# Decode attention on one core: scores of the next head before the PV of this one, K queued ahead of V, a replicated q layout, and a new start

## The chip, the cores and the metric

The kernel runs on one core of one Trainium2 chip. Times are device microseconds of a whole execution. The engines are called PE (matmul), PEld (weight load), DVE (vector), ACT (scalar), POOL (GpSimd) and SP (the sequencer that here issues nearly all DMAs).

## The reference

There are two independent blocks, A and B, with the same shapes; their outputs are joined. Each is one decode step of attention with a long cache:

```python
B, Sq, D = 8, 1, 1024;  H, Sk, Dh = 32, 4096, 128        # bf16
q = (x @ wq).reshape(B, Sq, H, Dh).transpose(0, 2, 1, 3)
scores = einsum("bhqd,bhkd->bhqk", q, k_cache) * Dh ** -0.5
o = einsum("bhqk,bhkd->bhqd", softmax(scores), v_cache)
out = o.transpose(0, 2, 1, 3).reshape(B, Sq, H * Dh) @ wo
```

Every byte of K and V is used once: 2 x 2 x 8 x 32 tiles of 1 MB, 1024 MiB, plus 32 MiB of wq and wo.

## The kernel before

A "head" n (64 in all, both blocks in a row) is 8 batches. For each batch one K tile and one V tile of [128, 4096] bf16 (1 MB) are loaded. DVE transposes the K tile; PE makes scores from it (8 matmuls of 512 columns); after eight tiles there is one softmax for all eight batches; then PE does PV (8 matmuls a tile). All loads come from one in-order queue, SP:

```python
NK = 6; NT = 2; NV = 8; LEAD = 2        # K buffers, transposed K, V buffers, q groups ahead

# SP: the load queue
load_group(first[0])                     # wq, eight DMAs of 128 KB, rows of 1 KB
wait(sp, s_const, 1)                     # all GpSimd constants ready
for blk in range(NBLK):
    sp.dma_start(x_sb[0:Bsz, blk, :], blocks[blk][0][:, 0, :]).then_inc(s_x, 16)
for n in range(NH):
    for b in range(Bsz):                 # K of this head
        wait(sp, s_tr, t - NK + 1)       # the transpose that frees the slot
        sp.dma_start(knat[:, slot, :], kc[b, h]...).then_inc(s_kld[slot], 16)
    for G in groups_at.get(n, []): load_group(G)
    sp.dma_start(wo_sb[:, ws, :], wo[h * 128:(h + 1) * 128, :])...
    for b in range(Bsz):                 # V of this head
        wait(sp, s_pv, t - NV + 1)       # the PV that frees the slot
        sp.dma_start(vnat[:, slot, :], vc[b, h]...).then_inc(s_vld[slot], 16)

# POOL: ahead of s_const
pool.memset(x_sb[:], 0.0)                # 128 partitions, of which 8 are used
pool.memset(q_pad[:], 0.0)
pool.memset(lpad[:], 0.0)
... # the constants, ident among them, then s_const

# PE, for head n
scores(n); max, bias and sum matmuls of n; prep(n + 1); PV(n); transpose o; output projection
# ... cut: the code is inline, in this order

# ACT, eviction of PV and the output
act.wait_ge(s_pv, (n + 1) * Bsz)         # all eight PV tiles
for slot in range(2):
    act.activation(o_sb[:, slot, :], O_ps[slot], ACT.Identity, scale=rlo_sb[:, slot:slot + 1])
...
for c in range(NOC):                     # last head of a block: NOC = 2 copies
    act.activation(out_sb[32 * c:32 * c + 8, blk, :], OUT_ps[c], ACT.Identity)
```

## Time and profile before

| | before |
|---|---|
| median (4 runs before the prediction; 13 with those taken beside the changed kernel) | 2669.84 us; 2669.67 us |
| profiled span | 2667.8 us |
| PE / DVE / ACT busy | 75% / 48% / 10% |
| read from HBM | 1107.33 MB, 415 GB/s over the span |
| last V tile landed | 2660.23 us |

The table of the span in 40 equal slices comes first. A digit of 9 means that the mean of the 16 DMA engines was busy for 90% or more of the slice; GB/s is what they moved. The last line is the share of each engine in the chain of work that ended last.

```profile
DMA  9999999999999999999999999999999999999998
GB/s 371 418 420 421 417 421 417 421 420 416 420 416 420 421 417 420 415 421 420 415 420 417 421 419 416 420 413 420 419 419 421 414 421 414 419 420 418 421 421 349
...
DMA 80%; DVE 9%; SPq 7%; PE 2%; issue 1%; ACT 0%; POOL 0%; DVEq 0%; POOLq 0%; ACTq 0%
```

Between the first and the last slice the rate never leaves 413 to 421 GB/s. This kernel's engines idle at every softmax (38.5 to 41.8 us in the first head), and its DMA rate does not show it: it is bound by its loads. Both ends are lower. The start, cut into stretches of 2.5 us, shows why (start and end, length, busy us and instructions of five engines, granted PE clock, DMA share, GB/s):

```profile
0.00:2.50 2.50, 0.00 (x0) 0.00 (x0) 1.40 (x3) 0.00 (x0) 1.91 (x5) 1.00 0.18 45
2.50:5.00 2.50, 0.00 (x0) 0.00 (x0) 2.22 (x6) 0.00 (x0) 2.50 (x3) 1.00 0.86 262
5.00:7.50 2.50, 0.00 (x0) 0.00 (x0) 0.26 (x1) 0.00 (x0) 2.47 (x6) 1.00 0.36 113
7.50:10.00 2.50, 0.00 (x0) 0.00 (x0) 0.83 (x5) 0.00 (x0) 0.80 (x6) 1.00 0.05 13
10.00:12.50 2.50, 0.39 (x32) 0.33 (x32) 0.00 (x0) 1.50 (x2) 0.00 (x0) 1.00 0.93 315
12.50:15.00 2.50, 2.44 (x38) 0.96 (x39) 1.26 (x1) 0.23 (x2) 0.00 (x0) 1.00 1.01 426
```

POOL is busy with memsets until 8 us, SP waits for it with x and K behind, and the DMA falls to 13 GB/s. The last part, from the timeline (start, length, engine, line, operation), runs from the last V tile to the issue of the output:

```profile
2660.27 1.89 PE L372 MATMUL ps<-vnat,pq_sb 128*4 128x512 bf16 x8 [0.57 <-DMA vnat<-in_B_v_cache_dram]
2662.20 1.26 ACT L452 ACTIVATE o_sb<-ps,rlo_sb 128x512 bf16<-128x512 f32 x2 [15.23 <-PE ps L372]
...
2664.56 1.20 ACT L460 ACTIVATE out_sb<-ps 8x512 bf16<-8x512 f32 x2 [0.48 <-PE ps L394]
2665.79 0.63 ACTq L463 DMA_DIRECT2D out_dram<-out_sb  x2
```

### The profile page before, as it was taken

What the parts mean: (1) busy time and instruction counts of PE and PEld (TensorE: products, weight loads), DVE (VectorE), ACT (ScalarE), POOL (GpSimd) and SP (SyncE); (2) the same over time, 40 slices, a digit from 0 to 9 for tenths busy, and PEclk for the clock granted to TensorE, in tenths of its full rate; (3) what the DMA queues carried; (4) which work ended last, traced back from release to release, by engine and by line L of the source; (5) the groups of instructions that cost most, each with busy time, mean ns of one, the idle gap of its engine ahead of it and who ended that gap; (6) DMA issues with size and microseconds to landing.
All of it is one profiled execution on the core that took longest, in us unless ns stands there. A gap on an engine that the chain in (4) does not pass through costs nothing.

```text
span 2667.8 us, 26152 instructions
## 1 busy us (share of the span) xinstructions
PE 2010.0 (75%) x10880; PEld 729.4 (27%) x10880; DVE 1292.2 (48%) x781; ACT 263.2 (10%) x727; POOL 7.7 (0%) x17
## 2 busy tenths in 40 slices
PE   6777777777777777777777777777777777777777
PEld 2222222222222222222222222222222222222222
DVE  5453544545535445364453544535535355363553
ACT  1001100011000110110101101011010100101001
POOL 1000000000000000000000000000000000000000
PEclk9998999999989999999999999999999899999999
DMA  9999999999999999999999999999999999999998
GB/s 371 418 420 421 417 421 417 421 420 416 420 416 420 421 417 420 415 421 420 415 420 417 421 419 416 420 413 420 419 419 421 414 421 414 419 420 418 421 421 349
DMA packets 175316, 1109.09 MB, mean 416 GB/s; under 512 B 19504, under 2 KB 35920, under 8 KB 44128
## 3 DMA queue, kind: packets, MB, share of 16 engines
q1 hardware_dynamic: 175136, 1107.41, 100.5%
q8 instruction: 86, 1.41, 0.2%
q14 instruction: 30, 0.25, 0.0%
q10 hardware_dynamic: 64, 0.03, 0.0%
HBM read 1107.33 MB, written 0.03 MB: 415 GB/s over the span
## 4 chain that ended last, share of the span: by engine, by line
DMA 80%; DVE 9%; SPq 7%; PE 2%; issue 1%; ACT 0%; POOL 0%; DVEq 0%; POOLq 0%; ACTq 0%
DMA knat<-in_B_k_cache_dram 39%; DMA knat<-in_A_k_cache_dram 36%; DVE kt L249 9%; SPq L189 3%; DMA vnat<-in_B_v_cache_dram 3%; DMA vnat<-in_A_v_cache_dram 3%; SPq L171 2%; SPq L202 1%; PE ps L334 1%; PE ps L289 1%; PE ps L372 0%; SPq L197 0%; ACT o_sb L452 0%; POOL lpad L211 0%; PE ps L394 0%
## 5 line engine op out<-in xcount | busy, mean ns | idle before, releaser
L249 DVE STREAM_TRANSPOSE kt<-knat 128x2048 f32<-128x2048 f32 x512 | 1171.2, 2304 | 1119.1 <-DMA knat<-in_B_k_cache_dram 536.6
L334 PE MATMUL ps<-kt,lpad 128*128 128x512 bf16 x4096 | 1025.1, 395 | 227.0 <-DVE kt L249 225.4
L372 PE MATMUL ps<-vnat,pq_sb 128*4 128x512 bf16 x4096 | 848.0, 432 | 121.7 <-DMA vnat<-in_B_v_cache_dram 60.7
L334 PEld LDWEIGHTS ps<-kt,lpad 128*128 128x128 bf16 x4096 | 368.0, 99 | 876.2 <-DVE kt L249 445.5
L372 PEld LDWEIGHTS ps<-vnat,pq_sb 128*4 128x4 bf16 x4096 | 292.2, 94 | 647.4 <-issue 151.2
L452 ACT ACTIVATE o_sb<-ps,rlo_sb 128x512 bf16<-128x512 f32 x128 | 80.9, 683 | 881.6 <-PE ps L372 881.6
L437 ACT ACTIVATE bias_sb<-ps 128x1 f32<-128x1 f32 x64 | 11.0, 171 | 1363.5 <-PE ps L347 1363.5
L253 DVE TENSOR_REDUCE m_sb<-ps 128x1 bf16<-128x512 f32 x64 | 44.4, 694 | 128.7 <-PE ps L334 128.7
L383 PE MATMUL ps<-selrow,o_sb 128*128 128x4 bf16 x512 | 22.6, 166 | 86.9 <-ACT o_sb L452 86.9
L261 DVE STREAM_TRANSPOSE pq_sb<-e_sb 128x512 bf16<-128x512 bf16 x64 | 45.5, 712 | 83.7 <-ACT e_sb L441 83.7
L424 ACT ACTIVATE lpad<-ps 32x32 bf16<-32x32 f32 x256 | 77.9, 304 | 70.3 <-PE ps L306 65.6
L354 PE MATMUL ps<-l1m_sb,maskcg 128*32 128x2 f32 x512 | 16.4, 188 | 90.5 <-ACT l1m_sb L445 90.5
L342 PE MATMUL ps<-ident,m_sb 128*1 128x128 bf16 x64 | 13.9, 217 | 50.3 <-DVE m_sb L253 50.3
L383 PEld LDWEIGHTS ps<-selrow,o_sb 128*128 128x128 bf16 x512 | 17.0, 96 | 119.0 <-ACT o_sb L452 119.0
L441 ACT ACTIVATE e_sb<-ps,bias_sb 128x512 bf16<-128x512 f32 x64 | 44.0, 687 | 2.1
L289 PE MATMUL ps<-wq_sb,xT_sb 128*8 128x512 bf16 x128 | 37.8, 449 | 0.0
L394 PE MATMUL ps<-wo_sb,oT_sb 128*8 128x512 bf16 x128 | 24.9, 386 | 17.1 <-ACT oT_sb L456 17.1
L354 PEld LDWEIGHTS ps<-l1m_sb,maskcg 128*32 128x32 f32 x512 | 10.9, 117 | 96.0 <-ACT l1m_sb L445 96.0
L306 PE MATMUL ps<-ident,q_pad 128*32 128x8 bf16 x1024 | 17.4, 171 | 24.9 <-DVE rlo_sb L264 24.2
L347 PE MATMUL ps<-scalecol,negm 128*32 128x1 bf16 x256 | 12.0, 177 | 23.9 <-DVE negm L257 23.9
L257 DVE TENSOR_REDUCE negm<-ps 1x16 bf16<-1x128 f32 x64 | 18.0, 281 | 19.8 <-PE ps L342 19.8
L342 PEld LDWEIGHTS ps<-ident,m_sb 128*1 128x1 bf16 x64 | 5.1, 79 | 82.1 <-DVE m_sb L253 82.1
(37 smaller groups left out, 119.2 us busy)
## 6 DMA issues: line engine op xcount, KB each, us to landing
knat<-in_A_k_cache_dram SPq DMA_DIRECT2D x256, 1024.0 KB, 26.4
vnat<-in_A_v_cache_dram SPq DMA_DIRECT2D x256, 1024.0 KB, 20.8
knat<-in_B_k_cache_dram SPq DMA_DIRECT2D x256, 1024.0 KB, 26.5
vnat<-in_B_v_cache_dram SPq DMA_DIRECT2D x256, 1024.0 KB, 20.9
wq_sb<-in_A_wq_dram SPq DMA_DIRECT2D x64, 128.0 KB, 10.1
wo_sb<-in_A_wo_dram SPq DMA_DIRECT2D x32, 256.0 KB, 12.8
wq_sb<-in_B_wq_dram SPq DMA_DIRECT2D x64, 128.0 KB, 9.3
wo_sb<-in_B_wo_dram SPq DMA_DIRECT2D x32, 256.0 KB, 12.8
```

Source lines behind the costliest of these rows:

```text
L171: sp.dma_start(wq_sb[:, G % 2, ch, :], wq[ch * 128:(ch + 1) * 128, g * GW:(g + 1) * GW]).then_inc(s_wq[G % 2], 16)
L189: sp.dma_start(knat[:, slot, :], kc[b, h].rearrange("(p j) d -> p (j d)", p=128),).then_inc(s_kld[slot], 16)
L249: dve.transpose(kt[:, ts, :].bitcast(F32), knat[:, ks, :].bitcast(F32)).then_inc(s_tr, 1)
L253: dve.tensor_reduce(m1_sb[:], S_ps[par], axis=AX.X, op=ALU.max).then_inc(s_m1, 1)
L261: dve.transpose(pq_sb[:], e_sb[:]).then_inc(s_pq, 1)
L289: last = pe.matmul(q_ps[G % 2], lhsT=xT_sb[:, blk, ch, :], rhs=wq_sb[:, G % 2, ch, :], start=(ch == 0), stop=(ch == NCH - 1))
L334: last = pe.matmul(S_ps[par], lhsT=lpad[:, b, c, 2 - 2 * g:2 - 2 * g + 128], rhs=ktv[:, 16 * g:16 * g + 16, bq, :, e_], start=(b == 0 and ...
L372: last = pe.matmul(O_ps[slot][32 * cg:32 * cg + 4, :], lhsT=pq_sb[:, base:base + 97:32], rhs=vnat[:, vs, j0 * 128:(j0 + 4) * 128], start=( ...
L383: last = pe.matmul(oT_ps[:, slot * 4:slot * 4 + 4], lhsT=o_sb[:, slot, m * 128:(m + 1) * 128], rhs=selrow4[:, m, :], start=(m == 0), stop= ...
L424: act.activation(dst, src, ACT.Identity).then_inc(s_lp, 1)
L441: act.activation(e_sb[:], S_ps[par], ACT.Exp, bias=bias_sb[:], scale=SCALE, accum_out=l1_sb[:]).then_inc(s_exp, 1)
L452: act.activation(o_sb[:, slot, :], O_ps[slot], ACT.Identity, scale=rlo_sb[:, slot:slot + 1]).then_inc(s_oev, 1)
```

## The change

The stated intent is to let the engines work on two heads at a time: PE does the scores and the maximum of head n+1 before the PV of head n, K of head n+1 is queued ahead of V of head n, and q is laid out so that four matmuls instead of sixteen prepare a head. The same diff also changes the start, the wq loads and the end:

```diff
-NT = 2
-NV = 8
-LEAD = 2
+NT = 4
+NV = 6
+LEAD = 3
@@ buffers
-        x_sb = sb("x_sb", [128, NBLK, D], BF16)
+        x_sb = sb("x_sb", [8, NBLK, D], BF16)          # no zero fill needed
-        q_pad = sb("q_pad", [128, 2, GW], BF16)
+        q_rep = sb("q_rep", [128, 2, HPG, 4, 128], BF16)
-        rlo_sb = sb("rlo_sb", [128, 2], F32)           # likewise pq_sb: two of each now
+        rlo_sb = sb("rlo_sb", [128, 2, 2], F32)
@@ SP: wq in one DMA, x and K at once, K a head ahead
-                for ch in range(NCH):
-                    sp.dma_start(wq_sb[:, G % 2, ch, :],
-                                 wq[ch * 128:(ch + 1) * 128, g * GW:(g + 1) * GW]).then_inc(s_wq[G % 2], 16)
+                sp.dma_start(wq_sb[:, G % 2, :, :],
+                             wq.rearrange("(ch p) n -> p ch n", p=128)[:, :, g * GW:(g + 1) * GW]
+                             ).then_inc(s_wq[G % 2], 16)
-            load_group(first[0]); wait(sp, s_const, 1); x; K(0), V(0), K(1), V(1), ...   (abridged)
+            x; load_group(first[0]); K(0); then per n: K(n+1), wq, wo, V(n)                (abridged)
@@ POOL: only what is needed, ident first; ACT zeroes q_rep and lpad
@@ PE
+            for n in range(NH):
+                if n + 1 < NH:
+                    qk(n + 1)
+                    smax_a(n + 1)
+                for b in range(Bsz):
+                    pv(n, b)
+                if n + 1 < NH:
+                    smax_b(n + 1)
+                if n + 2 < NH:
+                    prep(n + 2)
+                otr(n)
+                outproj(n)
@@ ACT: each slot is evicted after its own four PV tiles; one output copy; eight small q copies
-                act.wait_ge(s_pv, (n + 1) * Bsz)
                 for slot in range(2):
+                    act.wait_ge(s_pv, m * Bsz + min(4 * (slot + 1), Bsz))
-                    for c in range(NOC):
-                        act.activation(out_sb[32 * c:32 * c + 8, blk, :], OUT_ps[c], ACT.Identity).then_inc(s_outsb, 1)
+                    act.activation(out_sb[0:npart, blk, :], ps[0:npart, 7, 0:OW], ACT.Identity).then_inc(s_outsb, NOC)
... # cut: fp32 operands in the max path, masks moved, PSUM banks renumbered
```

## The prediction

> **What bounds the kernel now.** The DMA engines. The 40-slice table shows DMA at 90% or more in every slice but the last, and 413 to 421 GB/s in all but the first (371) and last (349). 1107 MB come from HBM in 2667.8 us. In 2.5 us stretches around 1000 us, DMA share is 1.00 to 1.04 through three heads, softmax included; the only dip (385, 307, 400 GB/s, about 1 us lost) is a wq group with its 1 KB rows. The chain of waits is 80% DMA. The Trainium skill, "DMA: Bandwidth & Descriptors", section "Where 436 GB/s comes from", puts the fabric ceiling at 435 GB/s; the trace's 419 to 423 is close to it: nothing is left to win in the steady state.
>
> PE (75% busy), DVE (48%) and ACT (10%) have slack: a head needs about 41.5 us of DMA, against 8x1.9 us scores and 8x1.9 us PV on PE (31 us) and 8x2.31 us transposes on DVE.
>
> **What the change does, and what it is worth**
>
> 1. Head pipelining (scores of n+1 before PV of n, later reciprocal, two pq, NT 4): removes idle time around softmax (38.5 to 41.8 us in the timeline, about 3.4 us a head). It is hidden already: about 0 us.
> 2. K(n+1) queued before V(n), NV 8 to 6 (12 MB of slots instead of 14): V(n,6) can only be issued after PV(n,0), which I put about 8.4 us after the last K tile lands (transpose 2.3, scores 1.9, max/row/bias about 2, PV 1.9), with about 15 us of V queued. Some 6 us remain, so no steady bubble: 0 us.
> 3. Start. Before, x waits for GpSimd memsets until 8.4 us and K begins at 9.1 us; by 10 us only 1.08 MB have come (windows: 45, 262, 113, 13 GB/s): about 7.5 us lost. After, x, wq and K go at once; I expect saturation by 3 to 4 us. Gain about 4.5 us.
> 4. The start gives some back: ACT now zeroes q_rep and lpad (4096 and 4224 elements; at about 1 ns each, from 683 ns for 512, about 8 us) and makes eight q copies instead of one (about 3 us). Scores start at about 20 us, against 18.8. K tile 6 of head 1 waits for the first head's softmax, and V(0,6) for head 1's: two bubbles, about 3 us lost.
> 5. End: first-slot eviction overlaps PV, output copy is one instruction instead of two (0.59 us each): -1.2 us.
> 6. wq as one DMA: 7/8 of its semaphore packets vanish (1792 of 9.6 ns over 16 engines): -1 us. The 1 KB rows stay.
> 7. q layout (4 matmuls instead of 16), fp32 max path: off the path, 0 us.
>
> Sum: -4.5 + 3 - 1.2 - 1, about -4 us: **2666 us, range 2657 to 2674**. Faster by over 2%: 0.02; within 2%: 0.965; slower by over 2%: 0.015.
>
> **What would show it.** Right: first slice above 371 GB/s, middle slices still 413 to 421; waiting for DMA still DVE's main idle; chain still mostly DMA. Step 2 wrong: DMA share below 1.0 once per head at V tile 6, middle slices below 410. Step 4 wrong: no DMA dips between 35 and 70 us (then nearer 2662), or longer ones.
>
> **What would make it wrong.** The smaller V ring starving DMA each head (1 us per head is 64 us, 2.4%); the single strided wq DMA generating descriptors badly; another DMA rate from the new order.

## The result

| | before | after |
|---|---|---|
| median | 2669.67 us (13 runs) | 2662.54 us (2662.41 to 2663.26, 9 runs) |
| profiled span | 2667.8 us | 2660.8 us |
| PE / DVE / ACT busy | 75% / 48% / 10% | 77% / 49% / 11% |
| last V tile landed | 2660.23 us | 2654.22 us |

The medians differ by 7.1 us. The ratio is 0.9974, with a 95% interval of 0.9964 to 0.9983. A ratio is the mean time of one kernel's fast runs over that of the other's from the same rounds, so it is not quite the ratio of the medians. By the 2% mark the two kernels are the same. The prediction, 2666 us with 2657 to 2674, holds the result, but it foresaw about half of the difference, and the range of 17 us would have held the kernel before as well.

The 40 slices of the changed kernel, and its chain:

```profile
DMA  9999999999999999999999999999999999999998
GB/s 399 417 421 417 421 420 417 421 416 420 421 417 421 416 421 421 413 421 417 421 421 416 421 417 419 421 416 420 414 421 421 417 420 415 420 421 414 420 421 360
...
DMA 69%; DVE 12%; PE 11%; SPq 7%; issue 1%; ACT 0%; DVEq 0%; ACTq 0%
```

The middle is as it was, 413 to 421 GB/s. The first slice rose from 371 to 399. Its first 15 us, in the same stretches as before:

```profile
0.00:2.50 2.50, 0.00 (x0) 0.00 (x0) 1.39 (x3) 1.67 (x2) 1.78 (x16) 1.00 0.06 13
2.50:5.00 2.50, 0.38 (x32) 0.32 (x32) 0.06 (x1) 2.50 (x2) 0.13 (x1) 1.00 0.93 243
5.00:7.50 2.50, 0.82 (x34) 0.47 (x35) 0.00 (x0) 1.20 (x3) 0.00 (x0) 1.00 1.12 419
7.50:10.00 2.50, 2.50 (x7) 0.73 (x6) 0.57 (x1) 0.00 (x0) 0.00 (x0) 1.00 1.01 419
10.00:12.50 2.50, 0.64 (x2) 0.00 (x0) 2.32 (x2) 1.83 (x7) 0.00 (x0) 1.00 1.01 423
12.50:15.00 2.50, 0.58 (x5) 0.32 (x6) 2.43 (x7) 1.61 (x6) 0.00 (x0) 1.00 1.01 419
```

The full rate is there from 5 us on, where before it came at 12.5 us, and it stays: every stretch up to 85 us is at a DMA share of 1.00 or more. The end, in the timeline:

```profile
2654.27 1.89 PE L385 MATMUL ps<-vnat,pq_sb 128*4 128x512 bf16 x8 [0.56 <-DMA vnat<-in_B_v_cache_dram]
2656.20 0.69 ACT L492 ACTIVATE o_sb<-ps,rlo_sb 128x512 bf16<-128x512 f32 x1 [9.10 <-PE ps L385]
...
2658.09 0.59 ACT L505 ACTIVATE out_sb<-ps 40x512 bf16<-40x512 f32 x1 [0.54 <-PE ps L412]
2658.71 0.63 ACTq L508 DMA_DIRECT2D out_dram<-out_sb  x2
```

One eviction and one output copy are gone from the tail. From the last PV to the output's issue it is 4.44 us (2658.71 less 2654.27), where it was 5.52 us.

There is a finer way to see where a load-bound kernel gains: count the bytes of the load queue (x, wq, K, V and wo) that have arrived by a given time, from the packet records of the trace, and turn the lead over the kernel before into time at 419.5 GB/s. One trace stands for each kernel, and the lead is good to about 0.2 us.

| lead over before at | 40 us | 80 us | 1000 us | 2600 us |
|---|---|---|---|---|
| after | 4.5 us | 4.5 us | 4.8 us | 5.4 us |

So 4.5 of the 7.1 us are won in the first 40 us and are never given back, 0.9 us drift in over the next 2560 us, another 0.6 us before the last V tile lands 6.0 us earlier, and the last 1.1 us come from the tail just shown.

### The profile page after: what moved, and what is told of

The parts are those of the page before. It is cut to its first block, busy times and chain, and to the rows that moved or that the text cites. A ratio compares the mean times of both kernels' runs of the same rounds, so it can differ in the third digit from the quotient of the medians.

```text
span 2660.8 us, 24546 instructions
## 1 busy us (share of the span) xinstructions
PE 2054.7 (77%) x10048; PEld 749.1 (28%) x10048; DVE 1295.7 (49%) x776; ACT 298.8 (11%) x839; POOL 1.9 (0%) x16
## 4 chain that ended last, share of the span: by engine, by line
DMA 69%; DVE 12%; PE 11%; SPq 7%; issue 1%; ACT 0%; DVEq 0%; ACTq 0%
DMA knat<-in_B_k_cache_dram 31%; DMA knat<-in_A_k_cache_dram 30%; DVE kt L266 10%; PE ps L385 6%; DMA vnat<-in_B_v_cache_dram 5%; SPq L206 5%; PE ps L343 3%; DMA vnat<-in_A_v_cache_dram 3%; SPq L211 1%; SPq L184 1%; DVE m_sb L274 1%; PE ps L356 1%; DVE negm L280 1%; PE ps L361 0%; SPq L173 0%
## 5 line engine op out<-in xcount | busy, mean ns | idle before, releaser
L343 PE MATMUL ps<-kt,lpad 128*128 128x512 bf16 x4096 | 1012.4, 394 | 184.8 <-DVE kt L266 182.7
L385 PE MATMUL ps<-vnat,pq_sb 128*4 128x512 bf16 x4096 | 894.0, 380 | 212.0 <-DMA vnat<-in_A_v_cache_dram 106.6
L274 DVE TENSOR_REDUCE m_sb<-ps 128x1 f32<-128x512 f32 x64 | 44.3, 691 | 128.9 <-PE ps L343 128.9
L356 PE MATMUL ps<-identf,m_sb 128*1 128x128 f32 x128 | 24.3, 270 | 50.2 <-DVE m_sb L274 50.2
L457 ACT ACTIVATE q_rep<-ps 8x256 bf16<-8x256 f32 x128 | 35.5, 358 | 49.3 <-PE ps L310 49.3
L361 PE MATMUL ps<-scalecol,negm 128*32 128x1 f32 x512 | 15.5, 181 | 23.8 <-DVE negm L280 23.8
L280 DVE TENSOR_REDUCE negm<-ps 1x16 f32<-1x128 f32 x64 | 17.8, 279 | 30.2 <-PE ps L356 30.2
L370 PEld LDWEIGHTS ps<-l1m_sb,maskcg 128*128 128x128 f32 x128 | 19.0, 188 | 28.9 <-issue 27.4
L370 PE MATMUL ps<-l1m_sb,maskcg 128*128 128x2 f32 x128 | 24.5, 262 | 1.4 <-ACT l1m_sb L485 1.4
```

Of the source, the lines that this page charges most:

```text
L274: dve.tensor_reduce(m1_sb[:], S_ps[par], axis=AX.X, op=ALU.max).then_inc(s_m1, 1)
L280: dve.tensor_reduce(negm[0:1, :].rearrange("p (i x y) -> p i x y", i=8, x=2)[:, :, :, 0], r_in, axis=AX.XY, op=ALU.max, negate=True).then_ ...
L343: last = pe.matmul(S_ps[par], lhsT=lpad[:, b, c, 2 - 2 * g:2 - 2 * g + 128], rhs=ktv[:, 16 * g:16 * g + 16, bq, :, e_], start=(b == 0 and ...
L356: pe.matmul(R_ps, lhsT=m1_sb[:, 0:1], rhs=identf[:, :], start=True, stop=True).then_inc(s_row, 1)
L385: last = pe.matmul(O_ps[slot][32 * cg:32 * cg + 4, :], lhsT=pq_sb[:, m % 2, base:base + 97:32], rhs=vnat[:, vs, j0 * 128:(j0 + 4) * 128], ...
```

## The experiments

Medians are compared with the kernel before of the same session (2669.40 to 2669.54 us), or with the 2662.54 us of the changed kernel, which was not run again beside them: that comparison goes from one session to another, and the kernel before, run in all four, moved by less than 0.3 us (2669.40 to 2669.67 us). My theory was: the gain is the start, the end and the semaphore packets of wq. The rival: pipelining the heads gives a good part of it.

### All of the change without the pipelining

```diff
 # the kernel before, and only:
+x first, then wq in one DMA, K at once; x_sb of 8 partitions; ident made first
+first slot evicted after its own PV tiles; one output copy
```

> All of the change except the head pipelining: the kernel before with x, wq and K issued at once, wq as one DMA per group, first-slot eviction overlapped and one output copy. Theory A (the 7.1 us come from the start, about 4.5, the end, about 1.0, and the semaphore packets, about 1; pipelining is worth nothing under a saturated DMA): 2662.5 us, within 1.5. Rival B (the pipelining and the K-first order give a good part of the gain, and the start less): above 2665.

Measured: 2664.17 us (2664.03 to 2664.94), correct. This is 0.2 us outside what theory A allowed. Of the gain, 5.3 us come without any pipelining; 1.6 us are missing against the full change. Rival B, in the strong form that I gave it, is refuted.

### The pipelining alone

```diff
 # the changed kernel, and:
+wq first, wait for s_const behind 8 us of GpSimd memsets, then x and K
+wq in eight DMAs; evictions wait for all PV tiles; two output copies
```

> Only the head pipelining, the K-first order, NT 4, NV 6 and the q layout; the start (x after 8 us of GpSimd memsets, K behind it), wq as eight DMAs and the old end are put back. Theory A: 2669.7 us, within 1.5, as before. Rival B: below 2667.

Measured: 2668.58 us (2668.16 to 2668.99), correct, 0.9 us less than before in the same session, ratio 0.9996 (0.9983 to 1.001). Theory A's value was 2669.7 within 1.5. So the pipelining of 64 heads is worth about 1 us, some 0.04%: not quite the nothing that I predicted, and within the noise of the ratio. The bytes of the traces place it: this kernel is 0.5 us behind the kernel before at 40 us and 0.5 us ahead at 2600 us, while the one without pipelining keeps its lead (4.4 us, then 4.6). So the microsecond is won slowly, in the long middle; what wins it stays open.

### The old start alone

```diff
-            x; load_group(first[0]); K(0)
+            load_group(first[0]); wait(sp, s_const, 1); x; K(0)      # POOL: 8 us of memsets first
```

> The changed kernel with only the old order of the start: wq first, then x and K behind 8 us of GpSimd memsets; everything else stays. Theory (step 3): the bytes moved by 40 us fall by about 1.8 MB, 4.3 us of DMA, and the time rises by 4.5 us: 2667 us, within 1. Rival (the start is worth less, the rest comes from the steady state): below 2665.5.

Measured: 2667.53 us (2667.36 to 2667.92), correct, 5.0 us more than the changed kernel, as the theory had it. Its bytes at 40 us are 0.6 us behind the kernel before, where the changed kernel is 4.5 us ahead.

### The old end alone

```diff
+                act.wait_ge(s_pv, (m + 1) * Bsz)      # all eight tiles before either slot
-                    act.activation(out_sb[0:npart, blk, :], ps[0:npart, 7, 0:OW], ...)
+                    for c in range(NOC): act.activation(out_sb[32 * c:32 * c + 8, blk, :], ...)
```

> The changed kernel with only the old end: the first-slot eviction waits for all eight PV tiles, and two output copies. Theory (step 5): +1.0 to +1.2 us, 2663.7; the 64 evictions in between cost nothing. Rival (the evictions in every head also matter): above 2665.

Measured: 2663.96 us (2663.70 to 2664.00), correct: 1.4 us more. The tail is worth what it shows in the timeline, and the evictions inside the run hardly matter.

### wq in eight DMAs

```diff
-                sp.dma_start(wq_sb[:, G % 2, :, :], ...)
+                for ch in range(NCH): sp.dma_start(wq_sb[:, G % 2, ch, :], ...)
```

> The changed kernel with wq as eight DMAs per group again. Theory A: +1.1 us for 1792 semaphore packets and about +1 us because the first wq group is again bound by its issue (eight issues took 3.69 us before K): 2664.5 us, within 1. Rival (semaphore packets hide behind data and cost nothing): below 2663.3.

Measured: 2665.16 us, but with a spread of 2664.03 to 2668.38, correct. The median alone seems to confirm 2664.5; the bytes tell it apart. Against the changed kernel this one is already 1.7 us behind at 40 us (a lead of 2.8 instead of 4.5) and 2.0 us behind at 2600 us. So most of what can be placed is the first wq group, bound by its eight issues; the semaphore packets of the other fifteen groups cost about 0.3 us and not the 1 us that I had put down for them. The profiled run took 2665.91 us; the 1.4 us that it lost after 2600 us, and the spread, are not explained.

### The loads alone

```diff
-                    wait(sp, s_tr, t - NK + 1)
+                    wait(sp, s_kld[slot], 16 * (t // NK))     # likewise V, wq, wo
-        @block.vector, @block.tensor, ...
+        zeros to the output, once all loads have landed
```

> Every load of the changed kernel in its order into its slots, each only waiting for the previous load of its slot to land; no compute, output zeros (wrong on purpose). Theory A (DMA engines saturated, compute costs only the end): about 6.6 us less for the missing end, plus 2 us for the output store: 2657 us, within 2.5. Rival (bubbles or contention with the engines slow the loads in the steady state): below 2648.

Measured: 2652.12 us (2651.56 to 2652.98). This is 2.4 us below the range of theory A, and the rival's 2648 was not reached either: the steady state did leave something. The time even understates it. At 2600 us the loads alone are 9.3 us ahead of the changed kernel, but their last load lands only 6.6 us earlier (2647.2 against 2653.8 us): from 2642 us on, only one packet at a time is under way, where 16 were before. Most of the rest of the 10.4 us is the missing end. Its page has no instruction refills: where the changed kernel's page has the line

```profile
q8 instruction: 80, 1.31, 0.2%
```

(queue and kind, packets, MB, share), the page of the loads alone has only this, beside its loads:

```profile
q14 instruction: 9, 0.07, 0.0%
```

I split 2500 us of the three traces into stretches of 2 us and summed what each lost against 422 GB/s, the rate of an undisturbed stretch. (A row moves by up to 1 us with where the cuts fall, the sum of a column by 0.5 us.)

| lost in 2500 us | before | after | loads alone |
|---|---|---|---|
| stretches with wq packets (1 KB rows) | 13.4 us | 12.8 us | 10.7 us |
| with wo packets (2 KB rows) | 3.3 us | 2.7 us | 2.6 us |
| K and V only, within a stretch of a 16 KB instruction refill | 6.2 us | 6.0 us | none there |
| all other K and V | 0.8 us | 1.0 us | 0.4 us |

The instruction streams are loaded by the same DMA engines: 80 packets of 16 KB with 1.07 us each, 85.7 us over 16 engines, are 5.4 us. That fits the 6.0 us. The loads alone, which have no refills, also lack everything else that the engines do, and the number of instructions alone was not changed; so it is a reading and not a proof.

### A later start of the scores

The prediction had taken back 3 us for two bubbles near 40 and 60 us, because ACT's zero fills and eight q copies would delay the first scores to about 20 us. They began at 14.7 us, and no bubble came. These are the two zero fills, the eight q copies and the first scores in the trace of the changed kernel:

```profile
2.11 1.91 ACT L511 ACTIVATE q_rep<-q_rep 128x2048 uint32<-128x2048 uint32 x1
...
3.93 1.95 ACT L512 ACTIVATE lpad<-lpad 128x2112 uint32<-128x2112 uint32 x1
...
10.67 2.22 ACT L457 ACTIVATE q_rep<-ps 8x256 bf16<-8x256 f32 x8 [3.94 <-PE ps L310]
...
14.69 13.05 PE L343 MATMUL ps<-kt,lpad 128*128 128x512 bf16 x48 [1.47 <-ACT lpad L469]
```

If the bubbles were real and only the delay was mis-sized, restoring the delay must bring them:

```diff
             act.memzero(q_rep[:])
             act.memzero(lpad[:])
+            for i in range(3):                  # a second run with 6
+                act.memzero(zpad[:]).then_inc(s_late, 1)
+                act.wait_ge(s_late, i + 1)
```

> The changed kernel with three more zero fills of 1.95 us on ACT ahead of the first x copy, so that scores start near 20.5 us, where the prediction had put them, instead of 14.7. In the changed kernel K tile 6 of head 1 is issued at 38.2 us and V tile 6 of head 0 at 59.2 us, while the queue runs dry near 41.7 and 62.2 us by the landings. Theory: the first softmax ends about 3 us later, both issues come within a microsecond of the dry point, and 1 to 2 us are lost: 2664 us, DMA share dips once or twice between 40 and 65 us. Rival (the queue has more slack than I count): 2662.5, no dip.

Measured: 2665.87 us (2665.43 to 2667.20), correct: 3.3 us more than the changed kernel, so the theory's 1 to 2 us were too few, and the prediction's 3 us fit the delay that it had assumed (scores began at 20.4 us). The stretches of 2.5 us:

```profile
37.50:40.00 2.50, 0.70 (x12) 0.36 (x11) 0.83 (x2) 1.25 (x4) 0.00 (x0) 1.00 1.01 423
40.00:42.50 2.50, 0.37 (x7) 0.28 (x7) 2.50 (x4) 1.22 (x4) 0.00 (x0) 0.86 0.37 151
42.50:45.00 2.50, 2.50 (x7) 0.82 (x8) 2.50 (x2) 0.00 (x0) 0.00 (x0) 0.50 0.52 170
45.00:47.50 2.50, 2.50 (x13) 1.08 (x12) 2.50 (x2) 0.00 (x0) 0.00 (x0) 0.96 0.98 400
```

This is K tile 6 of head 1, which SP could issue only at 42.4 us, behind the first softmax on DVE. The two middle rows lack 3.1 us of transfer at 420 GB/s; after 60 us there is only a dip of a few tenths. So it is one bubble and not two.

> The same with six more zero fills, scores from about 26.5 us. Theory: K tile 6 of head 1 is issued some 5 us after the queue is dry: a bubble of about 7 us near 42 us and one of about 1 us near 65 us: 2670 us, within 2.5. Rival (slack larger, or later stages make up for it): below 2666.

Measured: 2672.15 us (2671.45 to 2672.43), correct: 9.6 us more, within the range. The bubbles lie elsewhere than the theory had them, though: besides some 6 us between 40 and 52 us there is one of 3 us before (161 and 167 GB/s from 30 to 35 us). Once the slack is used up, delay at the start is paid in full: the second 5.9 us of fill cost 6.3 us.

### Fewer V buffers

The prediction had claimed some 6 us of slack at V tile 6 of each head. In the trace of the changed kernel, the last K tile of a head has landed by the start of its transpose, and SP issues V tile 6 when the first PV is done:

```profile
1041.27 2.31 DVE L266 STREAM_TRANSPOSE kt<-knat 128x2048 f32<-128x2048 f32 x1 [0.17 <-DMA knat<-in_A_k_cache_dram]
...
1049.13 1.20 SPq L211 DMA_DIRECT2D vnat<-in_A_v_cache_dram  x2
```

The wait is 7.9 us (predicted 8.4), with six V tiles of 2.49 us and wo in the queue. To see whether that sum is the right one, it was driven to zero:

```diff
-NV = 6
+NV = 4        # a second run with 3
```

> The changed kernel with four V buffers instead of six. By the slack sum of step 2, V tile 4 of a head is issued about 7.9 us after the last K tile landed (read from the trace now), with four V tiles and wo queued, 10.6 us: 2.7 us left, about what a load needs to start. Theory: 0 to 1 us lost a head, so between 2662 and 2700 us, middle 2672. Rival (the sum is off by 3 us or more per head): over 2750.

> The changed kernel with three V buffers. Theory: V tile 3 is issued when only 8.1 - 7.9 = 0.2 us of loads are left, so the queue is dry for the 1.5 to 2 us that a load takes to start, once in each of 63 heads: 100 to 130 us lost, 2775 us, between 2720 and 2820, with one dip of the DMA share per head right after the first PV matmuls. Rival (V ring depth does not matter): 2663.

Measured: 2701.66 us (2697.94 to 2703.33) with four and 2882.33 us (2875.70 to 2885.09) with three, both correct. Over 63 heads that is 0.6 and 3.5 us a head. Both are above the theory's ranges, four only just. The cliff is where the sum puts it, but beyond it the loss is twice what I had. One head with three buffers:

```profile
1040.00:1042.50 2.50, 1.49 (x16) 0.65 (x18) 0.86 (x2) 0.77 (x3) 0.00 (x0) 1.00 0.71 292
1042.50:1045.00 2.50, 2.50 (x20) 1.00 (x16) 0.71 (x1) 0.47 (x3) 0.00 (x0) 1.00 0.19 33
1045.00:1047.50 2.50, 0.58 (x3) 0.08 (x1) 0.00 (x0) 0.00 (x0) 0.00 (x0) 1.00 0.99 406
1047.50:1050.00 2.50, 1.80 (x5) 0.61 (x6) 0.00 (x0) 0.00 (x0) 0.00 (x0) 0.58 0.99 419
1050.00:1052.50 2.50, 2.50 (x13) 0.86 (x10) 0.00 (x0) 0.69 (x1) 0.00 (x0) 0.74 0.98 413
1052.50:1055.00 2.50, 2.20 (x10) 0.62 (x8) 0.00 (x0) 0.00 (x0) 0.00 (x0) 1.00 0.90 305
1055.00:1057.50 2.50, 0.05 (x1) 0.00 (x0) 0.00 (x0) 0.00 (x0) 0.00 (x0) 1.00 0.77 285
```

The first gap is the one expected, but it costs 3 us: the packets under way fall from 16 to 4 at 1041.75 us, V tile 3 is issued at 1043.43 us, and 16 are under way again only 1.8 us later. Then comes a second: PE waits for that tile until 1048.2 us, resumes at a granted clock of 0.58 in this stretch, its PV takes 3.4 us instead of 1.9, and the next V slot is freed late, at 1051.6 us. How much of the second gap the clock alone costs was not tested.

### Longer wq rows

The 1 KB rows of wq lose most in the table above, so two runs load two and four groups per DMA:

```diff
-        wq_sb = sb("wq_sb", [128, 2, NCH, GW], BF16)
+        wq_sb = sb("wq_sb", [128, NCH, 4 * GW], BF16)          # 2 * GW in the other run
-                wait(sp, s_qps, G - 1)
+                if G % 4:
+                    return
+                wait(sp, s_qps, G)
-                             wq...[:, :, g * GW:(g + 1) * GW]
+                             wq...[:, :, g * GW:(g + 4) * GW]
```

> The changed kernel with wq loaded for two groups at a time, in rows of 2 KB instead of 1 KB. In the trace the stretches with wq rows lose 12.9 us against the rate around them, 0.86 us per MB, those with wo's 2 KB rows 0.18 us per MB. Theory (the row length costs it): 7 to 11 us less, 2653 us, within 3. Rival (the large row pitch of wq, or q work in these stretches): above 2660.

> The same for four groups at a time, rows of 4 KB. Theory: a little less than the pair, 2652 us, within 3; the first load is then 4 MB ahead of K, so scores start some 7 us later, and the queue goes dry as much later, so no bubble at 40 us. Rival: as for the pair, above 2660, or a bubble at the start that makes it slower than the pair.

Measured: 2658.48 us (2658.41 to 2658.62) with 2 KB rows and 2656.20 us (2655.63 to 2657.60) with 4 KB, both correct: 4.1 and 6.3 us less than the changed kernel, against about 9.5 and 10.5 expected. Neither lies in its range, nor where the rival had it. The direction is right, the size is not. The larger distance between wq's rows in HBM (8 KB, where wo's rows lie one behind the other) is hardly the reason: counted as in the table above, the stretches with rows of wq or wo lose 15.5 us in the changed kernel (12.8 and 2.7) and 8.1 us with 2 KB rows, 7.4 us less and within the theory. But the stretches with K and V only lose 10.2 us instead of 7.0. The place can be found: in the 3 us after each issue of V tile 6 this kernel loses 6.1 us over 61 heads, the changed kernel 3.1 us over 60. So part of what the rows won is lost again where the V ring is tightest. Why it is tighter with longer wq rows, and whether a seventh V buffer would help, was not tested. The second is the fastest kernel that computes the result here, 0.995 (0.9938 to 0.9963) of the kernel before.

## Why the prediction was right, and where it was off

- **The bound was right, its last sentence too strong.** The middle slices stayed at 413 to 421 GB/s, as predicted. But "nothing is left to win in the steady state" failed: the loads alone moved their first 1090 MB in about 9 us less than the changed kernel (a lead of 14.7 us at 2600 us against 5.4), and longer wq rows won 6.3 us.
- **Step 1, pipelining, "about 0 us": nearly right.** 0.9 us alone, 1.6 us on top of the rest, less than 0.03 us a head. The bytes place it in the steady state, which was to give nothing. The pipelined kernels have 80 instruction refills and not 86; by their duration six fewer would be 0.4 us of it, the rest stays open.
- **Step 2, no steady bubble: right for this kernel.** The wait was 7.9 us for 8.4, and fewer buffers show the cliff between six and four. The size beyond the cliff was wrong by two.
- **Step 3, start, "about 4.5 us": right.** The lead at 40 us is 4.5 us, and undoing the start cost 5.0 us. The full rate came at 5 us and not by 3 to 4.
- **Step 4, "about 3 us lost" to two bubbles: this is the term that failed**, and it is nearly all of the 3.5 us by which the prediction missed. The mechanism is real, with one bubble for two: with the scores held back by 5.7 us one of 3.1 us appears. The mis-sized term is ACT's time at the start. The zero fills took 1.91 and 1.95 us instead of 8 us in all, because the instructions in the trace write 4-byte elements (2048 and 2112 of them), and the eight q copies took 2.22 us instead of 3. Scores began at 14.7 us, not 20. The prediction had named this case: without the dips, "nearer 2662". That nothing else shows in the total is luck: about 1 us more from the pipelining and 0.7 us less from the semaphore packets nearly cancel.
- **Step 5, end, -1.2 us: right** (1.1 us in the timeline, 1.4 us by undoing it).
- **Step 6, wq semaphores, -1 us: too large.** About 0.3 us by the bytes; the single DMA helped more by getting the first group out at once, which step 3 already held.

## What to carry to other kernels

When the loads run at their full rate through every softmax, reordering the engines wins next to nothing (here about 1 us of 2670); look at the time before the first full-rate transfer, at the compute after the last landing, and at what else travels on the DMA engines. Slack in a buffer ring can be summed from the trace (time until the slot is freed against the loads still queued), and the sum says where the cliff is, though not how deep. Before charging a zero fill or a copy by its element count, find the width in which it will be written.

## What the Trainium skill lacked or had wrong

- "DMA: Bandwidth & Descriptors", section "Where 436 GB/s comes from", gives 435 GB/s for the fabric and says that for HBM to SBUF the HBM side, about 358 GB/s, binds. With this program on one core, these traces hold 413 to 421 GB/s in the middle slices, and 422 in an undisturbed stretch: the 358 did not bind. The sentence is too general rather than the page wrong: its own measurements for a single core reach 425 GB/s.
- "Runtime: NRT & Kernel Launch", section "Instruction fetch mechanics", says of a 16 KiB boundary that its cost is "one DMA tail-bump, mostly hidden". Here, with the DMA engines saturated, it does not look hidden: 80 refills of 16 KB in the changed kernel take 1.07 us each on an engine, and the stretches around them lose 6.0 us of 2500. This is the reading above, not tested alone.
- "DMA: Bandwidth & Descriptors", section "Specifications", names 512 B and more for line rate. Rows of 1 KB still cost: their packets took 49.7 ns on average, where 8 KB took 314 ns or 39 ns a KB, wq's stretches lost 12.8 us, and rows of 4 KB took 6.3 us off the time.
- No page that I used says that a zero fill of a bf16 tile on ACT runs as 4-byte elements: 2048 of them for 4096 values, 1.91 us. "VectorE: DVE Perf Modes", section "Zero memsets can be issued as uint32 (trn2)", says that zero fills can be issued so, but of VectorE's memset only.
